# Attention state in three column strips, border factors multiplied behind their transfer, scores cut at the causal mask

## The chip, the core and the metric

The kernel runs on one core of a Trainium2 chip. The metric is the device time in microseconds of one execution. TensorE is called PE here (its weight loads PEld), VectorE DVE, ScalarE ACT, GpSimd POOL, and SyncE, which issues all transfers, SP.

## What is computed

Three layers in a row. The first is a gated attention of 4 batches with 8 heads, 768 steps and a head size of 48. The other two are dense layers on the 3072 tokens (384 to 2048 to 384 with an elu, and 384 to three times 768, maximum, to 384). The change touches the first alone:

```python
S_re, S_im = 0, 0                        # a 48x48 state per head, complex
for t in range(S):
    new_re = ar * S_re - ai * S_im       # ar, ai: a_re, a_im with their length cut to 0.999
    new_im = ar * S_im + ai * S_re
    S_re, S_im = (new_re + k[t] (x) v[t], new_im)
    y[:, :, t] = q[t] @ S_re
```

## The kernel before

The steps of a batch are cut into 6 chunks of 128; two neighbouring chunks of all 8 heads are one group n (12 groups), its chunks c = 0 and 1, the second with its steps in reverse order. In a chunk the recurrence becomes matrix products. Phases and log lengths are summed over the steps, and from them come `ep` and `em` (exponentials of the summed log length and of its negative). `hat` (L444) turns q and k into `qh` and `kh` with 96 rows per head (cosine and sine parts).

- `score` (L499) multiplies kt and qt of each head: 128 x 128 values in a PSUM bank, four heads to a bank, so two halves `hf` per chunk. For n < PE_TR = 3 that is one matmul per head (L505). From n = 3 on the 128 key rows are four strips of 32 columns of the array (`tile_position`), because the transposed k lies in four blocks of 32 (L508). `mask` (L513) then multiplies the whole bank by `keep[c]`, which is 0 where the key is later than the query.
- `state` (L522) is one matmul per head, 96 columns of `kh` against 48 columns of v (L531). `state_out` (L540) adds it to the running state and multiplies by the factor `g`, which carries the decay over the border between two chunks.
- `gain` (L388) makes `g`: it takes the exponential `gt` of half a log length from `rate` (L382), multiplies it on DVE by `em` of the next chunk and `ep` of this one (L394, L395, on 32 partitions, though only one row is needed), writes the row to DRAM (`gd`, L398), and reads it back turned, one value per partition and head, twice (L401).
- `yout` (L554) adds masked scores times v and state times q, also in four column strips (L563).
- Scores, states, outputs and sums take their PSUM banks from `apsum` (L127): at the start of the kernel three banks "h" and two banks "a" in turn, later the two "a" alone.

Group n's steps are laid by a table (`STEPS`, L633) between the steps of the first dense layer: `h_pair` (L681) and `o_pair` (L724) give 18 + 18 matmuls per step, and `elu` and `elu_split` follow on ACT and DVE two steps behind. So PE alternates between long runs of L681 and L724 and short pieces of attention. A scheduler behind the program sets the final order on each engine; every engine works its own row strictly in that order, and SP issues all transfers in one row. The second dense layer (L928, L952) comes at the end and holds no attention.

Of the kernel before, what the change touches and what calls it, by code (L numbers as in the profile page):

```python
# [9 lines left out]
F32 = mybir.dt.float32  # L10
F32R = mybir.dt.float32r
# [3 lines left out]
AF = mybir.ActivationFunctionType  # L15
ALU = mybir.AluOpType
# [3 lines left out]
B, H, S, D = 4, 8, 768, 48  # L20
P = 128
W = H * D
NCH = S // P
NG = B * NCH // 2
# [9 lines left out]
NWA, NWB = 2 * DM, 3 * NK * P + DM  # L34
LAG = 2
PE_TR = 3
NCONST = 8 * P + 2
PRIO_X = 400
DEC0 = 2
RAW0 = 2  # L40
# [52 lines left out]
def tile_kernel(  # L93
# [14 lines left out]
    nc = tc.nc  # L108
    act = ActQueue(tc)
    cp = ctx.enter_context(tc.tile_pool(name="cp", bufs=1))  # L110
# [4 lines left out]
    ps = pm.enter_context(tc.tile_pool(name="ps", bufs=1, space=PSUM))  # L115
# [9 lines left out]
    early = [0, True]  # L125

    def apsum():  # L127
        if early[1]:
            early[0] += 1
            if early[0] % 5 not in (1, 3):  # L130
                return ps.tile([P, 512], F32, tag="h", name="a", bufs=3)
        return ps.tile([P, 512], F32, tag="a", name="a", bufs=2)

    def load_re(n):
        T["re", n] = at([P, 2, W], "re")
# [19 lines left out]
    sums_raw = at([P, 4 * P], "p", bufs=2)  # L155
    nc.sync.dma_start(sums_raw, consts[:, 3 * P + 2:7 * P + 2])
    sums_r = cp.tile([P, 4 * P], F32R, name="sums_r")
    nc.gpsimd.tensor_copy(sums_r, sums_raw)
    tri_l = [sums_r[:, i * P:(i + 1) * P] for i in (0, 1)]
    keep_r = [sums_r[:, i * P:(i + 1) * P] for i in (2, 3)]  # L160
    keep = [x.bitcast(F32) for x in keep_r]

    def const_col(x, name):
        t = cp.tile([P, 1], F32, name=name)
# [12 lines left out]
    gd = dp.tile([2 * NG, 1, W], F32, name="gd")  # L177

    def load_w(pool, src, f, n, tag):
        raw = pool.tile([P, n, 2], U32, tag=tag, name="raw")  # L180
# [50 lines left out]
        )  # L231
        return split_w(wpool, t, n, tag)

    s_tiles = [at([96, 4, P], f"s{i}") for i in (0, 1)]
    for s in s_tiles:
        nc.vector.memset(s, 0.0)

# [13 lines left out]
        nc.sync.dma_start(T["k", n], k[n])  # L251

    def load_v(n, c):
        T["v", n, c] = at([P, 512], "v", bufs=2)
        nc.sync.dma_start(T["v", n, c], v[n, :, c, :])

    def new(nm, n):
# [53 lines left out]
    def bslice(c):  # L311
        return slice(96, 128) if c == 0 else slice(0, 32)
# [67 lines left out]
        act.activation(em, bank[:, :W], AF.Exp, scale=-1.0)  # L380

    def rate(n):  # L382
        T["gt", n] = t = at([P, W], "gt")
        for c in (0, 1):
            sl = bslice(1 - c)
            act.activation(t[sl], T["lnr", n][sl, c, :], AF.Exp, scale=0.5)

    def gain(n, c):  # L388
        if ends(n, c):
            return  # L390
        n2, c2 = after(n, c)
        sl = bslice(c)
        t = T["gt", n2]
        nc.vector.tensor_tensor(out=t[sl], in0=t[sl], in1=T["em", n2, c2][sl], op=ALU.mult)  # L394
        nc.vector.tensor_tensor(out=t[sl], in0=t[sl], in1=T["ep", n, c][sl], op=ALU.mult)  # L395
        row = P - 1 if c == 0 else 0
        ci = 2 * n + c
        nc.sync.dma_start(gd[ci], t[row:row + 1, :])  # L398
        g = at([96, H], "g", bufs=2)
        for j in (0, 1):  # L400
            T["dma"] = nc.sync.dma_start(  # L401
                g[j * D:(j + 1) * D, :], gd[ci].rearrange("o (h d) -> d (o h)", h=H)
            )
        T["g", ci] = g

    def heads(t):
# [46 lines left out]
    def tr_pe(n, c, x, hf):  # L453

        if n >= PE_TR:
            return
        if ("qkt", n, c) not in T:
            if early[1] and c == 1:
                d = [mp.tile([96, H, P], F32, tag="g", name="qkt", bufs=LAG + 1) for _ in "qk"]
            else:  # L460
                d = at([96, 2, H, P], "qkt")
                d = [d[:, 0], d[:, 1]]
            T["qt", n, c], T["kt", n, c] = ([y[:, i, :] for i in range(H)] for y in d)
# [48 lines left out]

    def mask(n, c, hf):  # L513
        bank = T.pop(("sc", n, c, hf))
        t = at([P, 4, P], "p", bufs=2)
        T["p", n, c, hf] = t
        nc.vector.tensor_tensor(  # L517
            out=t, in0=bank.rearrange("p (i t) -> p i t", i=4),
            in1=keep[c].unsqueeze(1).to_broadcast([P, 4, P]), op=ALU.mult,
        )  # L520

    def state(n, c):  # L522
        ci = 2 * n + c
        if ends(n, c):
            return
        bank = apsum()
        kh = T["kh", n, c].rearrange("p h j d -> p h (j d)")
        vt = T["v", n, c]
        for h in range(H):
            o = (h // 2) * P + (h % 2) * 80  # L530
            nc.tensor.matmul(  # L531
                bank[:96, h * D:(h + 1) * D], lhsT=kh[:, h, :], rhs=vt[:, o:o + D],
                start=True, stop=True,
            )
        T["sps", ci] = bank

    def split_heads(t):
# [677 lines left out]
def _consts():  # L1215
    import numpy as np

    t = [np.arange(P), P - 1 - np.arange(P)]
    c = np.zeros((P, NCONST), np.float32)
    for i in (0, 1):  # L1220
        a, b = t[i][:, None], t[i][None, :]
        c[:, i * P:(i + 1) * P] = np.where(a <= b, -1 / (2 * np.pi), 0)
        m = np.zeros((P, P), np.float32)
        m[(b >= 64) & (a >= 64) & (a <= b)] = 0.5
        m[(b < 63) & (a > b) & (a <= 63)] = -0.5
        s = (3 + i) * P + 2
        c[:, s:s + P] = m
        c[:, s + 2 * P:s + 3 * P] = a <= b
    c[:, 2 * P:3 * P] = np.eye(P)
# [5 lines left out]
    return c  # L1235


def _row_perm():
# [11 lines left out]
def _layout(inputs):  # L1250
# [14 lines left out]
    vp[..., 80:96] = v[..., 1, 32:]  # L1265
    vp[..., 96:128] = v[..., 1, :32]
    a["v"] = vp.reshape(NG, P, 2, 4 * P)
# [50 lines left out]
```

## Time and profile before

| | |
|---|---|
| median of 3 runs (lowest to highest) | 940.64 us (939.47 to 941.17) |
| profiled execution, its own time | 941.66 us |
| its span | 939.7 us |
| mean granted clock of PE | 0.987 |
| PE, DVE, ACT, POOL busy | 899.0, 604.2, 536.8, 0.8 us |

Busy shares are averages over stages with different limits, so they are read by stretch. In the rows below a float32 matmul is two rows (two passes), and a matmul's length in the trace is longer than the distance to the next, since matmuls are pipelined; the distance between starts is what a matmul costs.

### The profile page before, as it was taken

The numbers are of one execution on the slowest core, as the hardware profiler recorded it, in microseconds if no ns is written. First come the engines' busy times: TensorE is split into PE (matmuls) and PEld (weight loads), VectorE is DVE, ScalarE is ACT, GpSimd is POOL, SyncE is SP. The second block draws the span as 40 slices with busy tenths as digits, with TensorE's granted clock in tenths as the row PEclk, the third lists the DMA queues.
The fourth block names the chain that finished last, engine by engine and source line by source line (L and its number), as shares of the span: only waits on it lengthen the run. The fifth ranks groups of instructions, "written<-read, shape, count | busy, mean of one in ns | idle before, by whom it ended". The sixth has DMA issues, their size and how long they took to land.

```text
span 939.7 us, 19152 instructions
## 1 busy us (share of the span) xinstructions
PE 899.0 (96%) x8036; PEld 820.3 (87%) x8036; DVE 604.2 (64%) x952; ACT 536.8 (57%) x869; POOL 0.8 (0%) x5
## 2 busy tenths in 40 slices
PE   4579999999999999999999999999999999999997
PEld 1568889999999999999999999998888889898886
DVE  6889899788777797877786743778843141322220
ACT  8868777776767675757564533655858521211111
POOL 0000000000000000000000000000000000000000
PEclk9987999999999999999999999999999999999999
DMA  8662012343333333333323221619687401000001
GB/s 312 230 244 63 1 47 80 79 114 96 81 81 96 80 97 100 78 91 86 83 62 92 51 57 42 252 39 367 220 308 277 151 2 67 1 26 9 18 17 38
DMA packets 69703, 99.41 MB, mean 106 GB/s; under 512 B 22740, under 2 KB 52584, under 8 KB 68840
## 3 DMA queue, kind: packets, MB, share of 16 engines
q1 hardware_dynamic: 69608, 98.10, 33.1%
q8 instruction: 65, 1.06, 0.5%
q14 instruction: 30, 0.25, 0.1%
HBM read 74.45 MB, written 9.47 MB: 89 GB/s over the span
## 4 chain that ended last, share of the span: by engine, by line
PE 85%; DVE 6%; ACT 4%; DMA 3%; issue 1%; SPq 0%; DVEq 0%; ACTq 0%
PE mb L928 21%; PE x L724 21%; PE h L681 20%; PE ob L952 7%; PE a L563 5%; PE a L508 4%; PE a L531 3%; DMA rng<-in_a_im_dram 2%; PE a L330 1%; PE a L505 1%; ACT rng L78 1%; PE a L468 1%; ACT L78 1%; ACT aux L78 1%; DMA g<-gd 1%
## 5 line engine op out<-in xcount | busy, mean ns | idle before, releaser
L681 PE MATMUL h<-x,w 128*128 128x256 f32 x1728 | 232.9, 286 | 4.9 <-ACT w L83 2.5
L724 PE MATMUL x<-g,w 128*128 128x256 f32 x1728 | 230.3, 286 | 1.8 <-ACT x L83 1.4
L681 PEld LDWEIGHTS h<-x,w 128*128 128x128 f32 x1728 | 217.9, 192 | 11.4 <-ACT w L83 3.4
L928 PE MATMUL mb<-xx,w 128*128 128x512 f32 x972 | 224.8, 392 | 0.0
L724 PEld LDWEIGHTS x<-g,w 128*128 128x128 f32 x1728 | 215.3, 191 | 9.8 <-issue 6.9
L928 PEld LDWEIGHTS mb<-xx,w 128*128 128x128 f32 x972 | 182.4, 188 | 40.8
L78 ACT ACTIVATE e<-h 128x512 f32<-128x512 f32 x96 | 57.1, 595 | 104.8 <-PE h L681 104.8
L692 DVE SCALAR_TENSOR_TENSOR e<-e,h 128x512 f32<-128x512 f32 x96 | 65.1, 678 | 42.5 <-ACT e L78 42.0
L83 ACT CAST g<-e 128x512 fp32r<-128x512 f32 x96 | 59.4, 618 | 52.1 <-DVE e L692 51.7
L936 DVE TENSOR_TENSOR t<-mb,t 128x512 f32<-128x512 f32 x36 | 24.8, 689 | 96.1 <-PE mb L928 96.1
L701 DVE TENSOR_TENSOR g<-e,g 128x512 fp32r<-128x512 f32 x96 | 65.7, 685 | 18.8 <-ACT g L83 18.4
L952 PE MATMUL ob<-w,m 128*128 128x384 f32 x432 | 76.7, 337 | 0.1
L952 PEld LDWEIGHTS ob<-w,m 128*128 128x128 f32 x432 | 75.5, 188 | 0.9 <-ACT o L83 0.4
L83 ACT CAST m<-t 128x512 fp32r<-128x512 f32 x36 | 22.3, 620 | 92.1 <-DVE t L937 92.0
L78 ACT ACT_TABLE_LOAD x54 | 69.3, 1283 | 1.7 <-PEq L1302 0.8
L78 ACT ACTIVATE e<-e 128x512 f32<-128x512 f32 x96 | 60.6, 633 | 2.2
L937 DVE TENSOR_TENSOR t<-mb,t 128x512 f32<-128x512 f32 x36 | 24.9, 690 | 34.6 <-PE mb L928 34.5
L517 DVE TENSOR_TENSOR p<-a,sums_r 128x512 f32<-128x512 f32 x48 | 32.6, 683 | 10.7 <-PE a L508 8.1
L940 DVE TENSOR_TENSOR m<-t,m 128x512 fp32r<-128x512 f32 x36 | 24.8, 690 | 22.7 <-ACT m L83 22.7
L508 PE MATMUL a<-qkt 96*32 96x128 f32 x1152 | 38.9, 276 | 0.0
L83 ACT COPY o<-ob 128x384 f32<-128x384 f32 x24 | 11.4, 476 | 45.4 <-PE ob L952 45.3
L563 PE MATMUL a<-p,v 128*32 128x128 f32 x768 | 35.1, 283 | 0.3 <-DVE p L517 0.2
(106 smaller groups left out, 986.8 us busy)
## 6 DMA issues: line engine op xcount, KB each, us to landing
qkt<-tb SPq DMA_DIRECT2D x216, 64.0 KB
raw<-in_wa_dram SPq DMA_DIRECT2D x16, 768.0 KB
again<-in_wa_dram SPq DMA_DIRECT2D x16, 768.0 KB
raw<-in_wb_dram SPq DMA_DIRECT2D x6, 1536.0 KB
v<-in_v_dram SPq DMA_DIRECT2D x24, 256.0 KB
q<-in_q_dram SPq DMA_DIRECT2D x12, 384.0 KB
k<-in_k_dram SPq DMA_DIRECT2D x12, 384.0 KB
x2d<-x SPq DMA_DIRECT2D x36, 128.0 KB
```

What stands on the lines that cost most here:

```text
L78: ins = self.nc.scalar.activation(out, in_, func, **k)
L83: self.nc.scalar.copy(out, in_)
L508: nc.tensor.matmul(o[32 * s:32 * s + 32], lhsT=k1[:, s], rhs=q1, start=True, stop=True, tile_position=(0, 32 * s),)
L517: nc.vector.tensor_tensor(out=t, in0=bank.rearrange("p (i t) -> p i t", i=4), in1=keep[c].unsqueeze(1).to_broadcast([P, 4, P]), op=ALU.mult,)
L531: nc.tensor.matmul(bank[:96, h * D:(h + 1) * D], lhsT=kh[:, h, :], rhs=vt[:, o:o + D], start=True, stop=True,)
L563: nc.tensor.matmul(bank[32 * quad:32 * quad + 32, o * P:(o + 1) * P], lhsT=lhs, rhs=rhs, start=start, stop=stop, tile_position=(0, 32 * quad),
L681: nc.tensor.matmul(bank[:, i * BT:(i + 1) * BT], lhsT=w[:, wi, wsl], rhs=xb[b][:, xi, kk, :], start=m == 0, stop=m == 8,)
L692: nc.vector.scalar_tensor_tensor(out=e, in0=e, scalar=-1.0, in1=bank, op0=ALU.add, op1=ALU.max)
L701: nc.vector.tensor_tensor(out=g[:, 1], in0=e, in1=g[:, 0].bitcast(F32), op=ALU.subtract)
L724: nc.tensor.matmul(x2[m], lhsT=w[:, wi, wsl], rhs=g[:, gi, i * BT:(i + 1) * BT], start=j + i + s == 0 and b > 1, stop=j == NP - 1 and i == ...
L928: nc.tensor.matmul(bank, lhsT=wbt[f][:, wt, o:o + P], rhs=x[:, xi, kk].rearrange("p c t -> p (c t)"), start=m == 0, stop=m == 8,)
L952: nc.tensor.matmul(bank[:, :DM], lhsT=mt[:, mi, ts], rhs=wbt[f][:, wt, NWB - DM:], start=f == 0 and s == 0, stop=f == NF2 - 1 and s == 2,)
```

## The change

1. **State.** Each head's 96 columns of `kh` become three column strips of 32, with their own `tile_position`. The values v of odd heads, which `state` reads, lie in a place of their own behind the 512 columns of a v tile (704 columns).
2. **Border factors.** The rows of `em`, `ep` and the rate are written to `gd` one by one, read back turned in one transfer per half (3 x 8 values per partition), and multiplied there, on 96 x 8 values. The rate lies in 32 unused partitions of the state tiles.
3. **Scores.** All groups use strips. From n = 1 on a strip is as wide as the mask keeps it: for c = 0 strip f has queries f to 3, for c = 1 queries 0 to f (in blocks of 32). In odd heads the key blocks stand in reverse order in the columns, with the mask and v's rows reversed to match, and the strips are issued in the order 0, 3, 1, 2 or 3, 0, 2, 1.
4. **Banks.** What a strip does not write stays as it was in the bank and is multiplied by 0 in `mask`. So the two banks "a" are kept for good (`apsum_a`), and two matmuls set them to zero at the start.

```diff
     def apsum():
...
-        return ps.tile([P, 512], F32, tag="a", name="a", bufs=2)
+        return apsum_a()
+
+    def apsum_a():
+
+        if not banks_a:
+            banks_a.extend(ps.tile([P, 512], F32, tag="a", name="a", bufs=2) for _ in (0, 1))
+        banks_a.reverse()
+        return banks_a[0]
...
-    s_tiles = [at([96, 4, P], f"s{i}") for i in (0, 1)]
+    s_full = [at([P, 4, P], f"s{i}") for i in (0, 1)]
+    s_tiles = [s[:96] for s in s_full]
+    rates = [s.rearrange("p a t -> p (a t)")[96:128, :W] for s in s_full]
...
     def load_v(n, c):
-        T["v", n, c] = at([P, 512], "v", bufs=2)
+        T["v", n, c] = at([P, NV], "v", bufs=2)
...
     def rate(n):
-        T["gt", n] = t = at([P, W], "gt")
         for c in (0, 1):
-            sl = bslice(1 - c)
-            act.activation(t[sl], T["lnr", n][sl, c, :], AF.Exp, scale=0.5)
+            act.activation(rates[c], T["lnr", n][bslice(1 - c), c, :], AF.Exp, scale=0.5)

     def gain(n, c):
...
-        nc.vector.tensor_tensor(out=t[sl], in0=t[sl], in1=T["em", n2, c2][sl], op=ALU.mult)
-        nc.vector.tensor_tensor(out=t[sl], in0=t[sl], in1=T["ep", n, c][sl], op=ALU.mult)
-        row = P - 1 if c == 0 else 0
+        row, off = (P - 1, 31) if c == 0 else (0, 0)
         ci = 2 * n + c
-        nc.sync.dma_start(gd[ci], t[row:row + 1, :])
-        g = at([96, H], "g", bufs=2)
+        for i, x in enumerate((T["em", n2, c2], T["ep", n, c])):
+            nc.sync.dma_start(gd[ci, i:i + 1], x[row:row + 1, :])
+        nc.sync.dma_start(gd[ci, 2:3], rates[c2][off:off + 1, :])
+        f = at([96, 3, H], "f", bufs=2)
         for j in (0, 1):
             T["dma"] = nc.sync.dma_start(
-                g[j * D:(j + 1) * D, :], gd[ci].rearrange("o (h d) -> d (o h)", h=H)
+                f[j * D:(j + 1) * D], gd[ci].rearrange("o (h d) -> d o h", h=H)
             )
+        g = at([96, H], "g", bufs=2)
+        nc.vector.tensor_tensor(out=g, in0=f[:, 0], in1=f[:, 1], op=ALU.mult)
+        nc.vector.tensor_tensor(out=g, in0=g, in1=f[:, 2], op=ALU.mult)
...
     def score(n, c, hf):
...
-            o, k1, q1 = bank[:, i * P:(i + 1) * P], kt[4 * hf + i], qt[4 * hf + i]
-            if n < PE_TR:
-                nc.tensor.matmul(o, lhsT=k1, rhs=q1, start=True, stop=True)
-                continue
-            for s in range(4):
+            k1, q1 = kt[4 * hf + i], qt[4 * hf + i]
+            for s in (0, 3, 1, 2) if (i + c) % 2 == 0 else (3, 0, 2, 1):
+                f = s if i % 2 == 0 else 3 - s
+                a, b = (0, 4) if n == 0 else (f, 4) if c == 0 else (0, f + 1)
                 nc.tensor.matmul(
-                    o[32 * s:32 * s + 32], lhsT=k1[:, s], rhs=q1, start=True, stop=True,
+                    bank[32 * s:32 * s + 32, i * P + 32 * a:i * P + 32 * b],
+                    lhsT=k1[:, f], rhs=q1[:, a:b], start=True, stop=True,
                     tile_position=(0, 32 * s),
                 )
...
     def state(n, c):
...
-            o = (h // 2) * P + (h % 2) * 80
-            nc.tensor.matmul(
-                bank[:96, h * D:(h + 1) * D], lhsT=kh[:, h, :], rhs=vt[:, o:o + D],
-                start=True, stop=True,
-            )
+            o = (h // 2) * P if h % 2 == 0 else 4 * P + (h // 2) * D
+            for j in range(3):
+                sl = slice(32 * j, 32 * j + 32)
+                nc.tensor.matmul(
+                    bank[sl, h * D:(h + 1) * D], lhsT=kh[:, h, sl], rhs=vt[:, o:o + D],
+                    start=True, stop=True, tile_position=(0, 32 * j),
+                )
...
         nc.tensor.matmul(t, lhsT=zero[:, :P], rhs=zero, start=True, stop=False)
+    for t in (apsum_a(), apsum_a()):
+        nc.tensor.matmul(t, lhsT=zero[:, :P], rhs=zero, start=True, stop=True)
```

Three places show how the instructions stand before and after. On PE, a half of the scores of n = 3 between two runs of the dense layer, before:

```order
L724 MATMUL x_1966<-g,w 128x256 x3
L724 MATMUL x_1967<-g,w 128x256 x3
L508 MATMUL a<-qkt 32x128 x16
L330 MATMUL a<-gs,sums_r 128x384 x2
L724 MATMUL x_1968<-g,w 128x256 x3
```

and after, the first of its four heads (the other three repeat the four widths):

```order
L742 MATMUL x_119<-g,w 128x256 x3
L742 MATMUL x_120<-g,w 128x256 x3
L742 MATMUL x_121<-g,w 128x256 x3
L522 MATMUL a<-qkt 32x128
L522 MATMUL a<-qkt 32x32
L522 MATMUL a<-qkt 32x96
L522 MATMUL a<-qkt 32x64
```

The same 16 matmuls stand at the same place, with 128, 32, 96 and 64 columns in place of 128 each.

On PE, a state of a later group, before:

```order
L508 MATMUL a<-qkt 32x128 x16
L681 MATMUL h<-x,w 128x256 x18
L531 MATMUL a<-v,kh 96x48 x8
L563 MATMUL a<-p,v 32x128 x4
L563 MATMUL a<-qkt,s_101 32x128 x4
```

and after:

```order
L742 MATMUL x_121<-g,w 128x256 x3
L549 MATMUL a<-v,kh 32x48 x24
L699 MATMUL h<-x,w 128x256 x18
L742 MATMUL x_119<-g,w 128x256 x3
L742 MATMUL x_120<-g,w 128x256 x3
```

Eight matmuls of 96 weight columns became 24 of 32, and here they stand alone between runs of the dense layer.

On DVE, around the border factor of a later group (`s` is the running state, L551/L569 adds to it and L552/L570 multiplies by g), before:

```order
L517 TENSOR_TENSOR p<-a,sums_r 128x512
L692 SCALAR_TENSOR_TENSOR e<-e,h 128x512
L394 TENSOR_TENSOR gt<-gt,em_4163 32x384
L551 TENSOR_TENSOR s_100<-a,s_101 96x4x2x48
L395 TENSOR_TENSOR gt<-gt,ep_4079 32x384
L701 TENSOR_TENSOR g<-e,g 128x512
L552 TENSOR_TENSOR s_100<-s_100,g 96x4x2x48
```

and after:

```order
L532 TENSOR_TENSOR p<-a,sums_r 128x512
L415 TENSOR_TENSOR g<-f 96x8
L710 SCALAR_TENSOR_TENSOR e<-e,h 128x512
L416 TENSOR_TENSOR g<-g,f 96x8
L453 TENSOR_TENSOR q<-q,ep_4421 128x384
L453 TENSOR_TENSOR k<-k,em_4422 128x384
L569 TENSOR_TENSOR s_103<-a,s_104 96x4x2x48
L719 TENSOR_TENSOR g<-e,g 128x512
L570 TENSOR_TENSOR s_103<-s_103,g 96x4x2x48
```

L394 and L395 stood ahead of a transfer whose result a later L552 used. L415 and L416 stand behind the transfer whose result L570 uses here, and L415, the first to wait for it, is five operations ahead of L569.

## Rows read from the trace of the kernel before

**Rows 1.** The page, part 1: busy us, share of the span, instructions.

```profile
PE 899.0 (96%) x8036; PEld 820.3 (87%) x8036; DVE 604.2 (64%) x952; ACT 536.8 (57%) x869; POOL 0.8 (0%) x5
```

**Rows 2.** Stretches: length; PE, PEld, DVE, ACT, POOL busy (count); granted clock; DMA share; GB/s.

```profile
0.00:200.00 200.00, 166.03 (x1491) 146.23 (x1492) 170.55 (x271) 152.83 (x231) 0.81 (x5) 0.95 0.39 131
200.00:633.40 433.40, 433.40 (x5142) 416.37 (x5142) 321.72 (x519) 267.58 (x427) 0.00 (x0) 1.00 0.32 87
633.40:939.70 306.30, 299.62 (x1406) 257.66 (x1404) 111.90 (x162) 116.34 (x214) 0.00 (x0) 0.99 0.32 115
```

**Rows 3.** The chain that ended last, its share by engine.

```profile
PE 85%; DVE 6%; ACT 4%; DMA 3%; issue 1%; SPq 0%; DVEq 0%; ACTq 0%
```

**Rows 4.** PE in order of time, one score half: start us, length us, line, shapes, count.

```profile
191.66 1.08 PE L508 MATMUL a<-qkt 96*32 96x128 f32 x32
192.68 0.39 PE L724 MATMUL x<-g,w 128*128 128x256 f32 x1
```

**Rows 5.** The same from 191.66, windows ending at 191.70, 191.82, 191.93; PEld at 191.80.

```profile
191.46 0.28 PE L724 MATMUL x<-g,w 128*128 128x256 f32 x1
191.66 0.32 PE L508 MATMUL a<-qkt 96*32 96x128 f32 x4
191.66 0.43 PE L508 MATMUL a<-qkt 96*32 96x128 f32 x8
191.66 0.54 PE L508 MATMUL a<-qkt 96*32 96x128 f32 x12
191.66 0.16 PEld L508 LDWEIGHTS a<-qkt 96*32 96x32 f32 x8
```

**Rows 6.** L508's group (busy us, mean ns); stretches with L508 alone, then L531 alone.

```profile
L508 PE MATMUL a<-qkt 96*32 96x128 f32 x1152 | 38.9, 276 | 0.0
0.00:200.00 200.00, 2.16 (x64) 1.62 (x64) 0.95 0.39 131
200.00:633.40 433.40, 36.75 (x1088) 27.62 (x1088) 1.00 0.32 87
...
0.00:200.00 200.00, 10.92 (x96) 10.91 (x96) 0.95 0.39 131
200.00:633.40 433.40, 20.86 (x224) 20.53 (x224) 1.00 0.32 87
```

**Rows 7.** Chain in order of time, one run of the dense layer: start us, us, what.

```profile
163.26 2.15 PE x L724 x18
```

**Rows 8.** PE in order of time, one state; between, the window ending at 222.53.

```profile
222.48 1.48 PE L531 MATMUL a<-v,kh 128*96 128x48 f32 x16
223.78 0.61 PE L724 MATMUL x<-g,w 128*128 128x256 f32 x3
...
222.48 0.29 PE L531 MATMUL a<-v,kh 128*96 128x48 f32 x2
```

**Rows 9.** PE in order of time, a score half of n = 2.

```profile
138.16 1.06 PE L505 MATMUL a<-qkt 96*128 96x128 f32 x8
138.97 0.60 PE L681 MATMUL h<-x,w 128*128 128x256 f32 x3
```

**Rows 10.** DVE groups: shapes, count, busy us, mean ns, idle before.

```profile
L394 DVE TENSOR_TENSOR gt<-gt,em 32x384 f32<-32x384 f32 x20 | 11.0, 549 | 0.4
L395 DVE TENSOR_TENSOR gt<-gt,ep 32x384 f32<-32x384 f32 x20 | 11.0, 549 | 0.4
...
L1016 DVE SCALAR_TENSOR_TENSOR flags<-flags,sums 128x24 f32<-128x24 f32 x1 | 0.2, 184 | 4.1 <-ACT rng L78 4.1
```

**Rows 11.** Reads of g: chain at the start; PE's wait; SP and DVE around 175 us.

```profile
37.63 6.16 DMA g<-gd
...
44.52 3.75 PE L505 MATMUL a<-qkt 96*128 96x128 f32 x16 [4.31 <-DVE s L548]
...
174.15 2.08 SPq L401 DMA_DIRECT2D g<-gd  x2
...
178.08 0.55 DVE L548 TENSOR_TENSOR s<-a,g 96x384 f32<-96x384 f32 x1 [0.71 <-DMA g<-gd]
```

More of the change, by code (lines that the diff above doesn't have):

```diff
@@ L36 @@
 PE_TR = 3
-NCONST = 8 * P + 2
+NCONST = 10 * P + 2
+NV = 4 * P + 4 * D
 PRIO_X = 400
@@ L123, in at @@
         return ap.tile(shape, dt, tag=tag, name=name or tag, bufs=bufs)
-    early = [0, True]
+    early, banks_a = [0, True], []
     def apsum():
@@ L154, in tile_kernel @@
     wrap_at = cst[:, 3 * P:3 * P + 2]
[L155 to L161, printed above, removed]
+    sums_r = cp.tile([P, 6, P], F32R, name="sums_r")
+    for i in (0, 2):
+        raw = at([P, 4 * P], "p", bufs=2)[:, :(4 - i) * P]
+        a, b = (3 * P + 2, 7 * P + 2) if i == 0 else (8 * P + 2, 10 * P + 2)
+        nc.sync.dma_start(raw, consts[:, a:b])
+        nc.gpsimd.tensor_copy(sums_r[:, i + i:4 + i].rearrange("p a t -> p (a t)"), raw)
+    tri_l = [sums_r[:, i] for i in (0, 1)]
+    keep_r = [sums_r[:, i] for i in (2, 3)]
+    keep = [
+        sums_r[:, 2 + c::2].bitcast(F32).unsqueeze(1).to_broadcast([P, 2, 2, P]) for c in (0, 1)
+    ]
     def const_col(x, name):
@@ L176, in tile_kernel @@
     x2d = dp.tile([NT // P, P, NK * P], F32, name="x2d")
-    gd = dp.tile([2 * NG, 1, W], F32, name="gd")
+    gd = dp.tile([2 * NG, 3, W], F32, name="gd")
     def load_w(pool, src, f, n, tag):
@@ L391, in gain @@
         n2, c2 = after(n, c)
-        sl = bslice(c)
-        t = T["gt", n2]
-        nc.vector.tensor_tensor(out=t[sl], in0=t[sl], in1=T["em", n2, c2][sl], op=ALU.mult)
-        nc.vector.tensor_tensor(out=t[sl], in0=t[sl], in1=T["ep", n, c][sl], op=ALU.mult)
-        row = P - 1 if c == 0 else 0
+        row, off = (P - 1, 31) if c == 0 else (0, 0)
         ci = 2 * n + c
-        nc.sync.dma_start(gd[ci], t[row:row + 1, :])
-        g = at([96, H], "g", bufs=2)
+        for i, x in enumerate((T["em", n2, c2], T["ep", n, c])):
+            nc.sync.dma_start(gd[ci, i:i + 1], x[row:row + 1, :])
+        nc.sync.dma_start(gd[ci, 2:3], rates[c2][off:off + 1, :])
+        f = at([96, 3, H], "f", bufs=2)
         for j in (0, 1):
             T["dma"] = nc.sync.dma_start(
-                g[j * D:(j + 1) * D, :], gd[ci].rearrange("o (h d) -> d (o h)", h=H)
+                f[j * D:(j + 1) * D], gd[ci].rearrange("o (h d) -> d o h", h=H)
             )
+        g = at([96, H], "g", bufs=2)
+        nc.vector.tensor_tensor(out=g, in0=f[:, 0], in1=f[:, 1], op=ALU.mult)
+        nc.vector.tensor_tensor(out=g, in0=g, in1=f[:, 2], op=ALU.mult)
         T["g", ci] = g
@@ L462, in tr_pe @@
                 d = [d[:, 0], d[:, 1]]
-            T["qt", n, c], T["kt", n, c] = ([y[:, i, :] for i in range(H)] for y in d)
+            T["qt", n, c], T["kt", n, c] = (
+                [y[:, i, :].rearrange("p (s t) -> p s t", s=4) for i in range(H)] for y in d
+            )
             T["qkt", n, c] = d
@@ L517, in mask @@
         nc.vector.tensor_tensor(
-            out=t, in0=bank.rearrange("p (i t) -> p i t", i=4),
-            in1=keep[c].unsqueeze(1).to_broadcast([P, 4, P]), op=ALU.mult,
+            out=t.rearrange("p (i e) t -> p i e t", e=2),
+            in0=bank.rearrange("p (i e t) -> p i e t", i=2, e=2),
+            in1=keep[c], op=ALU.mult,
         )
@@ L529, in state @@
         for h in range(H):
-            o = (h // 2) * P + (h % 2) * 80
-            nc.tensor.matmul(
-                bank[:96, h * D:(h + 1) * D], lhsT=kh[:, h, :], rhs=vt[:, o:o + D],
-                start=True, stop=True,
-            )
+            o = (h // 2) * P if h % 2 == 0 else 4 * P + (h // 2) * D
[4 more added lines that the diff above has]
+                    start=True, stop=True, tile_position=(0, 32 * j),
+                )
         T["sps", ci] = bank
@@ L1228, in _consts @@
         c[:, s + 2 * P:s + 3 * P] = a <= b
+        c[:, (8 + i) * P + 2:(9 + i) * P + 2] = (a <= b)[_blocks()]
     c[:, 2 * P:3 * P] = np.eye(P)
@@ L1235, in _consts, with _blocks @@
     return c
+def _blocks():
+    import numpy as np
+    return np.arange(P).reshape(4, 32)[::-1].reshape(P)
 def _row_perm():
@@ L1264, in _layout @@
     vp[..., 0:48] = v[..., 0, :]
-    vp[..., 80:96] = v[..., 1, 32:]
-    vp[..., 96:128] = v[..., 1, :32]
-    a["v"] = vp.reshape(NG, P, 2, 4 * P)
+    odd = np.concatenate([v[..., 1, 32:], v[..., 1, :32]], axis=-1)
+    vp[..., 80:128] = odd[:, _blocks()]
+    a["v"] = np.concatenate(
+        [vp.reshape(NG, P, 2, 4 * P), odd.reshape(NG, P, 2, 4 * D)], axis=-1
+    )
     w_in = inputs["moe_w_in"][_row_perm()].reshape(NK, P, NF1, P).transpose(1, 2, 0, 3)
```

## The prediction

> **What bounds the kernel now.** I read the busy shares first: PE is busy for 899.0 of 939.7 us [rows 1]. An average over stages can hide a different limit in one of them, so the second view cuts the span in three. From 200 to 633.4 us PE is busy 433.40 of 433.40 us with a granted clock of 1.00 (the 2.4 GHz level), while DVE is busy 321.7 and ACT 267.6. Before 200 us PE has 166.0 of 200 and DVE 170.6. After 633.4 us nothing that the change touches is left [rows 2]. The chain that ended last is 85% PE and 6% DVE [rows 3]. So from 200 us on, a microsecond of PE work removed is a microsecond of the time, as long as PE stays the latest. Before 200 us DVE and transfers count as much as PE.
>
> The sums are made against the profiled execution, 941.66 us for a span of 939.7; that is 1.0 us above the median of the three runs, 940.64, so the result has 1.0 us taken off.
>
> **The score strips (L508).** A half of a chunk's scores is 4 heads x 4 strips x 2 rows, since each float32 matmul appears as two rows of the trace. One half: the last ordinary matmul starts at 191.46, L508 at 191.66, the next line at 192.68 [rows 4, 5]. Inside, four matmuls have started by 191.70, eight by 191.82, twelve by 191.93 [rows 5]: the four strips, which lie in four column groups, run side by side, in rounds. The last start is at 191.66 + 1.08 - 0.28 = 192.46 [rows 4, 6], so the 8 rounds are 0.81/7, about 0.11 us apart, 0.88 in all; the other 0.14 of the 1.02 us is the fill at the start and the way out. Ordinary rows follow each other every 2.15/18 = 0.12 us [rows 7]. L508 starts 0.08 later than that after its predecessor, and the way out after the last round costs 0.10: some 0.19 us for going into the strips and back.
>
> After the change a strip has 128, 96, 64 or 32 columns, and the next head gives the long strip to the column group that had the short one. Over two heads each group gets 4 + 1 or 3 + 2 blocks of 32 columns, twice: 10 blocks where it had 16. If each group works at its own pace and its time goes by columns, 0.88 becomes 0.55; I take 0.57, because short strips leave some weight loads uncovered. Saved per half: 0.31 us. No row shows a four-group burst with fewer than 128 columns, so this is bounded: from 0.33 saved to nothing saved (the feed, first rival). I take the upper part because a group's second matmul does not hold up its neighbours: the first round's four starts and all 8 weight loads of two rounds lie within 0.16 us [rows 5], and a 48-column row of L531 is followed by the next start within 0.05 us where the weights are there already [rows 8]. There are 1088 rows from 200 us on [rows 6], 34 halves of 32: 34 x 0.31 = 10.5 us, and 2 halves before that, 0.6.
>
> The groups n < 3 had whole 128x128 scores: 8 rows, 0.81 us to the next line [rows 9], 0.93 with the 0.12 before. As strips for n = 1 and 2 they cost 0.20 to enter + 0.57 + 0.14 = 0.91: nothing. For n = 0 the strips are full: 0.20 + 1.02, which is 0.29 more for each of 4 halves, at a place where PE waits anyway. I count zero; with no cover it is +1.2.
>
> **The state (L531).** Before: 16 rows of 96 weight columns, 1.30 us from first start to the next line [rows 8]; the starts are 1.30/16, about 0.08, apart although a 48-column row needs 0.05 or less: the weights set the pace. After: 48 rows in three column groups, 16 one after the other in each, at 48/128 x 0.11 = 0.042 us: 0.67, plus fill and way out 0.14, plus 0.09 for going in: 0.90. Saved: 0.40 each. Before, this matmul needed no change into column groups, so here the change adds 20 such returns at 0.19. The Trainium skill, page "TensorEngine Tiling (Array Packing)", section "Key Properties", speaks against this edit too: changing the tiling mode drains the engine. It gives no price; rows 4 and 5 do, and the 0.40 is what is left after paying it. The 224 rows after 200 us [rows 6] are 14 calls: 5.6 us. Of the 6 before, three lie where PE is nearly full (after 100 us): 1.2. Per call the bounds are 0.49 saved (no way in to pay, where it stands next to other strips) and 0.17 lost (first rival).
>
> **The border factors (L394, L395).** Two DVE operations of 550 ns go, 20 times each: 22 us. Two on 96x8 come; the nearest row is 184 ns for 128x24 [rows 10], so 7.4 us. From 200 us on DVE has over 100 us free, so 0. Before that 6 of the 20 are affected: 6 x 0.73 = 4.4 us of DVE work, of which I count 2.5, since PE or transfers are the later ones in part of it.
>
> Each factor now makes three small writes instead of one, and each of the two reads has 24 elements per partition instead of 8. They leave on SP's queue, in front of the loads of q, k, v and, at the start, of eight weight tiles. The new DVE operations wait for this read, and everything behind them on DVE waits too: the carry into th, the weight decode, e and g of the elu. Bounds: a read landed 6.16 us after its issue when the weight tiles followed it, and within 1.9 us (issued until 176.23, used at 178.08) elsewhere [rows 11]. Three times the elements takes between the same and three times as long: +0 to +12.3 at the start, +0 to +3.8 elsewhere. Against this, the writes no longer wait for two DVE operations (1.1 us), and the order puts the multiplications three or more DVE operations before the first use. At the start PE waited 4.31 us for L548 [rows 11]; in the new order the scores of the second chunk stand ahead of that wait. I take +1.5 at the start and 0 elsewhere. The wider v loads (704 columns for 512) and the two zeroing matmuls lie beside idle queues and an idle PE in the first 15 us: 0; uncovered they would be under 2 us each.
>
> **Sum.** -10.5 - 0.6 - 5.6 - 1.2 - 2.5 + 1.5 = -18.9 on 941.66, or 922.8; less 1.0 is 921.8, which I give as **922 us**.
>
> **Rivals.**
> *The feed.* In rows 4 the 32 matmuls start over 0.81 us, 0.026 each. The same number would come out if PE could not feed a weight load and a matmul faster than one pair in 0.026 us, whatever the columns. Then a score half saves nothing, a state is 48 x 0.026 + 0.23 = 1.47 for 1.30, and the halves of n = 1, 2 cost 0.29 more each: +0.17 x 17 + 0.29 x 12 - 2.5 + 1.5 = +5.4 at the most, about +2 with what PE idle covers before 200 us: 943. The edits together break even at some 0.025 us a pair. For it: the coincidence of the numbers. Against it: the first starts in rows 5, far closer together. A page has the same rule: the Trainium skill, "TensorE: Matmul & The Clock Gate", section "Wait — 56ns, not 53.3ns?", says that start to start never drops below about 25 ns however small the matmul. By that rule the result is about 941; the four starts within 0.04 us [rows 5] disagree for different column groups, and no run here shows it for a long burst. Chance 17%.
> *The read stalls DVE (slower).* If the read's time triples, the first one lands 12.3 us later and the other five before 200 us some 2.9 us later (3.8 less part of the 1.1), where DVE has little room: +27 against -17.9: about 950. It turns the sign once the six waits come to 18 us, 3 us each. For it: the only long wait for g in the trace is there. Against it: the reads go out before the weight loads and SP finds the rows ready earlier. Chance 12%.
> *PE is no longer last.* With 16 us less PE work from 200 us on, DVE is at 322 - 10 of 417 us, 75%, but in order, and e and g wait for ACT. If half of the gain is taken by such waits: 930. Chance 13%.
> The forecast has the other 58%.
>
> **How the numbers follow.** The forecast's own spread, from the bounds of the two PE terms and of the start, is 913 to 929. The range reaches up over the partial case and the feed to 943 and leaves out the stalled read and a little below: **913 to 943**. About 0.2%, 1.9 us, is what a measurement can tell from no change. Faster by more: forecast 58 + partial 13 + 4 of the feed's 17 = 75%. Within: 10% of the feed's. Slower: 12 + 3 = 15%.
>
> **What would show it.** Right: a score half (L522) goes from 1.02 us to about 0.70 from its first start to the next line, a state (L549) from 1.30 to about 0.81 with 0.20 before it, and the stretch from the first full PE window to the end of the h and x stage is 16 us shorter with PE still full. Feed: starts in L522 keep a mean of 0.026 us and L549 takes about 1.4 us. Stalled read: DVE rows of L415 with waits of several us for f. Wrong altogether: PE idle time in the stage that is full now, or a granted clock below 1.00 there.

## The result

The changed kernel takes 925.04 us (median of 4 runs, 923.73 to 925.48); the kernel before, on the same chip, 940.9. The ratio is 0.9838, with a 95% interval of 0.982 to 0.9855. The profiled execution took 924.66 us for a span of 922.9, so 17.0 us less than the one before, where the forecast was 18.9 less.

These lines of the profile after answer to [rows 1 to 3]: busy shares, the three stretches (the second ends where the dense stage ends now), and the chain that ended last.

```profile
PE 879.2 (95%) x8968; PEld 797.4 (86%) x8968; DVE 584.8 (63%) x952; ACT 535.8 (58%) x869; POOL 1.2 (0%) x6
...
0.00:200.00 200.00, 165.92 (x2001) 141.10 (x2002) 166.68 (x276) 153.45 (x233) 1.15 (x6) 0.94 0.46 143
200.00:616.50 416.50, 413.95 (x5565) 398.56 (x5564) 306.23 (x515) 266.47 (x424) 0.00 (x0) 1.00 0.37 92
616.50:922.90 306.40, 299.34 (x1406) 257.71 (x1404) 111.88 (x162) 115.90 (x214) 0.00 (x0) 0.99 0.32 115
...
PE 81%; ACT 9%; DVE 6%; issue 1%; SPq 1%; DMA 1%; DVEq 0%; ACTq 0%
```

PE is busy 19.8 us less, and the third stretch is as long as it was: all of the gain lies ahead of it. But PE is no longer busy for the whole of the second stretch: 2.55 us of it are idle, where there were none.

A score half and a state after 200 us, PE in order of time (start us, length us), answer to [rows 4] and [rows 8]:

```profile
226.62 0.76 PE L522 MATMUL a<-qkt 96*32 96x128 f32 x32
227.31 0.39 PE L742 MATMUL x<-g,w 128*128 128x256 f32 x1
...
219.52 0.88 PE L549 MATMUL a<-v,kh 128*32 128x48 f32 x48
220.34 0.51 PE L742 MATMUL x<-g,w 128*128 128x256 f32 x2
```

From the first start to the next line a half takes 0.69 us (1.02 before), a state 0.82 (1.30). Counted from the start of the ordinary matmul ahead to the start of the one behind, a half is 0.900 where it was 1.220, and a state 1.02 where it was 1.42; 28 of the stage's 34 halves and 12 of its 14 states show these figures to 0.01 us (33 and 11 in the trace of before).

The multiplications of the border factors, by group (count, busy us, mean ns, idle before them), answer to [rows 10] and [rows 11]:

```profile
L415 DVE TENSOR_TENSOR g<-f 96x8 f32<-96x8 f32 x20 | 3.1, 157 | 3.6 <-DMA f<-gd 3.5 <-issue 0.2
L416 DVE TENSOR_TENSOR g<-g,f 96x8 f32<-96x8 f32 x20 | 3.0, 148 | 0.0
```

In all 20 uses together DVE waited 3.5 us for the wider read.

Where PE is idle between 200 and 300 us (the bracket gives the idle time and what ended it):

```profile
209.68 0.84 PE L549 MATMUL a<-v,kh 128*32 128x48 f32 x45 [1.21 <-ACT em L79]
...
274.20 0.76 PE L522 MATMUL a<-qkt 96*32 96x128 f32 x32 [0.67 <-DVE nr L364]
...
278.38 0.45 PE L344 MATMUL a<-gs,sums_r 128*128 128x384 f32 x1 [0.62 <-DVE gs L334]
```

Each is a wait for the gate chain of a later group (angles, cumulative sums, their exponentials) on ACT and DVE.

### The profile page after: what moved, and what is told of

It is laid out like the page before. It is cut to its first block, busy times and chain, and to the rows that moved or that the text cites. A ratio compares the mean times of both kernels' runs of the same rounds, so it can differ in the third digit from the quotient of the medians.

```text
span 922.9 us, 21089 instructions
## 1 busy us (share of the span) xinstructions
PE 879.2 (95%) x8968; PEld 797.4 (86%) x8968; DVE 584.8 (63%) x952; ACT 535.8 (58%) x869; POOL 1.2 (0%) x6
## 4 chain that ended last, share of the span: by engine, by line
PE 81%; ACT 9%; DVE 6%; issue 1%; SPq 1%; DMA 1%; DVEq 0%; ACTq 0%
PE mb L948 24%; PE x L742 19%; PE h L699 18%; PE ob L972 8%; PE a L581 4%; PE a L522 3%; ACT L79 3%; ACT aux L79 1%; PE a L549 1%; PE a L344 1%; ACT e L79 1%; SPq L508 1%; ACT m L79 1%; PE a L483 1%; ACT g L84 1%
## 5 line engine op out<-in xcount | busy, mean ns | idle before, releaser
L742 PE MATMUL x<-g,w 128*128 128x256 f32 x1728 | 230.4, 286 | 0.5 <-DVE g L719 0.5
L948 PE MATMUL mb<-xx,w 128*128 128x512 f32 x972 | 224.8, 392 | 0.0
L742 PEld LDWEIGHTS x<-g,w 128*128 128x128 f32 x1728 | 215.1, 191 | 6.6 <-issue 3.8
L948 PEld LDWEIGHTS mb<-xx,w 128*128 128x128 f32 x972 | 182.4, 188 | 40.8
L522 PE MATMUL a<-qkt 96*32 96x128 f32 (+3 forms) x1536 | 38.0, 244 | 3.0 <-ACT qkt L84 2.3
L522 PEld LDWEIGHTS a<-qkt 96*32 96x32 f32 x1536 | 32.3, 112 | 9.5 <-ACT qkt L84 2.6
```

The lines of the kernel that those rows point to most:

```text
L522: nc.tensor.matmul(bank[32 * s:32 * s + 32, i * P + 32 * a:i * P + 32 * b], lhsT=k1[:, f], rhs=q1[:, a:b], start=True, stop=True, tile_pos ...
L742: nc.tensor.matmul(x2[m], lhsT=w[:, wi, wsl], rhs=g[:, gi, i * BT:(i + 1) * BT], start=j + i + s == 0 and b > 1, stop=j == NP - 1 and i == ...
L948: nc.tensor.matmul(bank, lhsT=wbt[f][:, wt, o:o + P], rhs=x[:, xi, kk].rearrange("p c t -> p (c t)"), start=m == 0, stop=m == 8,)
```

## Experiments

Four kernels ran beside each other in each of three groups, each group on one chip beside the kernel before. I compare by the ratio to the kernel before; 0.001 is 0.94 us. The kernel after, run again, gives the ratio to compare with: 0.9842 (0.9824 to 0.9859). The intervals reach 1.1 to 1.9 us either way, so differences of 1 or 2 us between two kernels are not clear of them.

### What sets the time of a score half

*Full strips* (kernel after, nothing skipped):

```diff
-                a, b = (0, 4) if n == 0 else (f, 4) if c == 0 else (0, f + 1)
+                a, b = 0, 4
```

> The kernel after, but every score strip is 128 columns wide again (nothing is skipped; the reversed blocks, the state in three strips and the new factors stay). Own pace: each column group runs through its own queue and its time goes by its columns, so a half (L522) goes from 0.69 us back to about 1.01 from its first start to the next line; 34 halves from 200 us on give +10.9 us, less up to 2.5 us of PE idle time between 200 and 300 us that slower scores would cover, and 8 halves of n = 1, 2 add 0 to 2.5: 933.5 to 938 us. Feed (the number of weight loads sets the time and the columns do not): halves stay near 0.69, 925 us.

Measured: 938.43 us, ratio 0.9989 (0.9975 to 1.0003). *No reversal* (skipping kept, but one column group has all the long strips; the layout of v and the mask follow):

```diff
-                f = s if i % 2 == 0 else 3 - s
+                f = s
...
-    vp[..., 80:128] = odd[:, _blocks()]
+    vp[..., 80:128] = odd
```

> The kernel after with the skipped columns, but odd heads are not reversed, so that one column group has the long strip (128 columns) of all four heads of a half and another the short one (32). The number of columns is that of the kernel after. Own pace: the slowest group has 16 blocks of 32 columns where it had 10, a half takes about 1.0 us again and the whole gain of the scores goes: 933.5 to 938 us, as in the run with full strips. Shared stream (the sum of the columns over all groups sets the time): a half stays at 0.69 us, 925 us.

Measured: 935.92 us, ratio 0.9973 (0.9961 to 0.9985). One half of each, PE in order of time, full strips first:

```profile
341.87 1.08 PE L522 MATMUL a<-qkt 96*32 96x128 f32 x32
342.88 1.34 PE L699 MATMUL h<-x,w 128*128 128x256 f32 x9
```

```profile
340.27 1.06 PE L522 MATMUL a<-qkt 96*32 96x128 f32 x32
341.26 1.94 PE L699 MATMUL h<-x,w 128*128 128x256 f32 x14
```

1.01 us with full strips, 0.99 with as many columns as in the kernel after but unevenly spread, 0.69 in the kernel after. With the sum of columns setting the time, the second would have been 0.69. So the busiest column group decides: 16 blocks of 32 columns in either slow case, 10 in the kernel after. The feed falls with the same rows, since the number of strips is the same in all three. By the ratios the first run is 0.0147, or 13.8 us, above the kernel after. 44 halves are affected (34 after 200 us, 10 before): 44 x 0.32 = 14.1, less 1.0 us that PE is idle less between 200 and 300 us, is 13.1. The second is 12.3 above: 44 x 0.30 = 13.2, less 1.5, is 11.7. The first is a little above what was expected, the second in its upper part; the sums fit if the halves before 200 us count in full.

*Order of issue* (kernel after, strips of each head issued as 0, 1, 2, 3):

```diff
-            for s in (0, 3, 1, 2) if (i + c) % 2 == 0 else (3, 0, 2, 1):
+            for s in range(4):
```

> The kernel after, but the four strips of every head are issued in the order 0, 1, 2, 3 where the kernel after changes the order from head to head; which group has which width is the same. If a group takes its next strip as soon as it is free, wherever that stands in the program: a half stays at 0.69 us, and the time at 0.984 of before. If strips have to start in the order of the program, a short strip waits behind the long one of the next head in another group: a half takes 0.75 to 1.0 us, 3 to 12 us more.

Measured: 929.59 us, ratio 0.989 (0.9877 to 0.9904), 4.5 us above the kernel after. The first theory is right about the half and wrong about the time. A half that stands in one piece takes 0.91 us from start to start instead of 0.90, so strips do not wait in the order of the program. But the scheduler, which here orders PE's rows anew, cut four of the 48 halves into 12 pieces with dense work between. One of them, in order of time:

```profile
294.81 0.25 PE L522 MATMUL a<-qkt 96*32 96x32 f32 x2
294.99 0.98 PE L699 MATMUL h<-x,w 128*128 128x256 f32 x6
295.90 0.30 PE L522 MATMUL a<-qkt 96*32 96x64 f32 x2
296.13 1.09 PE L699 MATMUL h<-x,w 128*128 128x256 f32 x7
297.15 0.35 PE L522 MATMUL a<-qkt 96*32 96x96 f32 x2
297.43 0.38 PE L699 MATMUL h<-x,w 128*128 128x256 f32 x1
...
298.34 0.75 PE L522 MATMUL a<-qkt 96*32 96x128 f32 x26
299.02 0.38 PE L742 MATMUL x<-g,w 128*128 128x256 f32 x1
```

The four pieces cost 0.39 + 0.44 + 0.49 + 0.89 = 2.21 us from start to start; less 0.90 for a whole half and three ordinary spacings of 0.12, each cut costs 0.32. Eight cuts are 2.5 us and 34 x 0.01 another 0.3; the other 1.7 I did not trace.

### The state

*Whole state* (kernel after, 96 weight columns at a time):

```diff
-            for j in range(3):
-                sl = slice(32 * j, 32 * j + 32)
...
-                    bank[sl, h * D:(h + 1) * D], lhsT=kh[:, h, sl], rhs=vt[:, o:o + D],
-                    start=True, stop=True, tile_position=(0, 32 * j),
+            nc.tensor.matmul(
+                bank[:96, h * D:(h + 1) * D], lhsT=kh[:, h, :], rhs=vt[:, o:o + D],
```

> The kernel after, but the state is one matmul with 96 weight columns per head again, as before. If the three strips give 0.40 us per call (0.81 + 0.21 us against 1.30 + 0.12): +5.6 us for the 14 calls from 200 us on, 0 to +2 for those earlier, less what PE idle time between 200 and 300 us swallows: 928 to 932.5 us. If the return into column groups eats it, or if PE waits elsewhere for as long: 924 to 926.

Measured: 928.07 us, ratio 0.9892 (0.9875 to 0.991), 4.7 us above the kernel after; a state is as before, and PE's idle time between 200 and 300 us is 1.36 us:

```profile
217.48 1.48 PE L547 MATMUL a<-v,kh 128*96 128x48 f32 x16
218.78 2.40 PE L740 MATMUL x<-g,w 128*128 128x256 f32 x18
...
200.00:300.00 100.00, 98.64 (x1246) 94.53 (x1248) 77.77 (x137) 70.72 (x109) 0.00 (x0) 1.00 0.39 91
```

14 x 0.40 = 5.6, less the 1.2 us that PE is idle less, is 4.4 for the 4.7 measured: the strips' gain is real, and part of it had turned into waits.

### The border factors

*Old factors* (kernel after, multiplied before the transfer, in the tile that holds the rates now):

```diff
-        for i, x in enumerate((T["em", n2, c2], T["ep", n, c])):
-            nc.sync.dma_start(gd[ci, i:i + 1], x[row:row + 1, :])
+        nc.vector.tensor_tensor(out=t, in0=t, in1=T["em", n2, c2][sl], op=ALU.mult)
+        nc.vector.tensor_tensor(out=t, in0=t, in1=T["ep", n, c][sl], op=ALU.mult)
+        nc.sync.dma_start(gd[ci], t[off:off + 1, :])
...
-        nc.vector.tensor_tensor(out=g, in0=f[:, 0], in1=f[:, 1], op=ALU.mult)
-        nc.vector.tensor_tensor(out=g, in0=g, in1=f[:, 2], op=ALU.mult)
```

> The kernel after, but the border factors are multiplied before the transfer again (two DVE operations on 32 x 384, one row written, 8 elements per partition read). By the forecast's steps (-2.5 us of DVE work before 200 us, +1.5 for the read at the start) this is +1.0: 924.5 to 927.5 us. If the 3 us that are missing to the forecast were lost to the larger transfers or to the waits of DVE for them: 922 to 923.5 us.

Measured: 924.26 us, ratio 0.9851 (0.9833 to 0.9869): 0.8 us above the kernel after, inside the intervals. That fits the forecast's +1.0, but it would fit no difference as well; the places do not agree. PE busy in three stretches, old factors first, then the kernel after:

```profile
0.00:100.00 100.00, 75.10 (x895) 55.77 (x896) 84.95 (x136) 81.14 (x118) 1.21 (x6) 0.91 0.57 206
100.00:200.00 100.00, 92.94 (x1102) 86.69 (x1101) 87.86 (x141) 74.97 (x118) 0.00 (x0) 0.97 0.29 79
200.00:300.00 100.00, 99.80 (x1444) 95.22 (x1447) 83.80 (x140) 72.91 (x114) 0.00 (x0) 1.00 0.34 88
```

```profile
0.00:100.00 100.00, 69.17 (x844) 50.08 (x845) 81.83 (x135) 75.52 (x113) 1.15 (x6) 0.88 0.60 207
100.00:200.00 100.00, 96.75 (x1160) 91.02 (x1159) 84.85 (x142) 77.94 (x122) 0.00 (x0) 1.00 0.32 79
200.00:300.00 100.00, 97.49 (x1399) 92.96 (x1398) 78.64 (x138) 71.87 (x112) 0.00 (x0) 1.00 0.37 88
```

With the new factors PE is busy 5.9 us less in the first 100 us, 3.8 more in the second, and 2.3 less in the third. Busy time is not progress where the clock differs (0.91 and 0.88, 0.97 and 1.00 here), so I also compare the starts of one row: the first x matmul starts at 75.21 us with old factors and at 82.38 in the kernel after, the 289th at 182.44 and 185.09, the first of the last stage at 615.17 and 616.30. The old factors start earlier and lose most of the lead again by 200 us. The idle time between 200 and 300 us goes with the new factors: with the same fast strips and old factors it is 0.20 us.

*New factors alone* (kernel before, only the factors changed):

```diff
-        nc.vector.tensor_tensor(out=t[sl], in0=t[sl], in1=T["em", n2, c2][sl], op=ALU.mult)
-        nc.vector.tensor_tensor(out=t[sl], in0=t[sl], in1=T["ep", n, c][sl], op=ALU.mult)
+        for i, x in enumerate((T["em", n2, c2], T["ep", n, c])):
+            nc.sync.dma_start(gd[ci, i:i + 1], x[row:row + 1, :])
```

> The kernel before with the new border factors alone (three rows written as they come, 24 elements per partition read, the two multiplications on 96 x 8 behind). By the forecast's steps -1.0 us against before (-2.5 of DVE work, +1.5 at the start): -3 to +0.5. If the factors cost at the start what they give between 100 and 200 us: within 1 us of before, with the marks at 100 us later than before and the difference gone by 200 us. If the larger reads hold DVE up: +3 us or more, and waits of several us for f.

Measured: 943.27 us (940.54 to 947.43 in 8 runs), ratio 1.0039 (1.002 to 1.0059): 3.4 us slower than before, outside the forecast's range. That is the size of the third case but not its cause: the waits for f are 6.1 us in 6 places, the longest 1.7. The profiled execution was the fastest of the eight, 1.1 us under the profile of before, so it does not show where the others lose. One number exists for all: the granted clock, averaged over the span, was 0.982 in the mean of the eight, against 0.989 in the mean of the 13 of the kernel before beside them. What part of the 3.4 us that is stays open; the mean clock does not order the kernels, for it was 0.981 in the next one, the fastest of its group.

*Two early old factors* (kernel after; n = 0 as in the run with old factors):

```diff
+    def gain_0(n, c):
...
+        if 2 * n + c < 2:
+            gain_0(n, c)
+        else:
+            gain_1(n, c)
```

> The kernel after, but the first two border factors (n = 0) are multiplied before the transfer, as before, and all later ones behind it. In the run with old factors throughout, the first elu work began 4 to 5 us earlier than in the kernel after and the lead was gone by 200 us, which I put down to the 549 ns multiplications that stand in DVE's way there. If so, this keeps the early start without the later loss: 2 to 5 us faster than the kernel after. If the early start came from the order of the whole program, or if DVE takes it back whatever the factors: within 1 us.

Measured: 922.22 us (920.95 to 923.82), ratio 0.9809 (0.9791 to 0.9826). The kernel after beside it: 925.02 (923.87 to 927.02), 0.9842 (0.9824 to 0.9859). That is 2.8 us faster, at the low end of what was expected, and the intervals only just touch. *The wide read alone* (that kernel, its two early factors still multiplied first, but written three times and read with 24 elements):

```diff
-        nc.sync.dma_start(gd[ci, 0:1], t[off:off + 1, :])
-        g = at([96, H], "g", bufs=2)
+        for i in range(3):
+            nc.sync.dma_start(gd[ci, i:i + 1], t[off:off + 1, :])
+        f = at([96, 3, H], "f", bufs=2)
...
```

> The kernel with the early old factors (0.981 of before), whose two early border factors are still multiplied before the transfer, but three rows are written and 24 elements per partition read for them, as in the kernel after; the program reads the first 8. This is the price of the wider transfers at the start by itself, apart from when the multiplications stand. By the forecast's +1.5 us: 0.9825 of before. If the read is what costs the kernel after its start: 0.984, with a wait of several us for f in the first use. If the width costs nothing: 0.981, and the first use waits no longer than with 8 elements.

Measured: 921.46 us (920.08 to 922.99), ratio 0.9809 (0.9795 to 0.9822): the width costs nothing that can be measured. With intervals of 1.3 and 1.7 us either way the times alone do not exclude the forecast's +1.5; the trace has to say whether anything waited. The first read and its first use on DVE, with no wait ahead of it:

```profile
34.73 1.04 SPq L411 DMA_DIRECT2D f<-gd  x2
...
43.06 0.55 DVE L588 TENSOR_TENSOR s<-a,f 96x384 f32<-96x384 f32 x1
43.52 0.94 DVE L216 TENSOR_TENSOR w<-dt,w 128x768 fp32r<-128x768 f32 x1
```

In the kernel after, the same place on DVE:

```profile
44.26 0.15 DVE L415 TENSOR_TENSOR g<-f 96x8 f32<-96x8 f32 x1
...
44.86 0.15 DVE L416 TENSOR_TENSOR g<-g,f 96x8 f32<-96x8 f32 x1
...
45.81 0.54 DVE L566 TENSOR_TENSOR s<-a,g 96x384 f32<-96x384 f32 x1
...
47.15 0.95 DVE L216 TENSOR_TENSOR w<-dt,w 128x768 fp32r<-128x768 f32 x1
```

Nothing waits for the transfer here either. But the state update and the first weight tile stand 2.8 and 3.6 us later, behind weight decoding that came after them in the other order, and the first h starts at 50.58 us where it starts at 46.35 in the run with the wide read. So at the start it is the order on DVE that costs, and the transfer makes nothing wait.

*The kernel after again*, unchanged:

> The kernel after, unchanged, beside the other three on one chip, so that differences of 1 to 3 us can be read. Every theory: 0.9838 of the kernel before (0.982 to 0.9855). If the PE idle time between 200 and 300 us and the gap of 5.7 us at 66 us are set by the order of the program, they stand at the same places again.

Measured: 925.02 us, ratio 0.9842. The gap before L549 stands in its trace again, 1.21 us for em, and PE has 97.33 of 100 us between 200 and 300. The gap at 66 us is there too, 6.96 us long where it was 5.70. These waits belong to the order.

### Whole scores at the start

*Early whole* (kernel after; scores and states of n < 3 as before, v and mask of these groups unreversed):

```diff
+            if n < PE_TR:
+                nc.tensor.matmul(
+                    bank[:, i * P:(i + 1) * P], lhsT=k1.rearrange("p s t -> p (s t)"),
+                    rhs=q1, start=True, stop=True,
+                )
+                continue
...
```

> The kernel after, but the first three groups (n < 3, up to about 200 us) have whole 128 x 128 scores and whole 96-column states, as before; odd heads are reversed from n = 3 on only. If the strips at the start are among what is missing to the forecast (the full strips of n = 0 cost 0.29 us a half, four halves): 1 to 2.5 us faster than the kernel after. If other work covers them there, as the forecast had it, and the states of n = 1, 2 give 0.40 us each: within 1 us, or up to 1.5 us slower.

Measured: 923.53 us, ratio 0.9825 (0.9805 to 0.9845): 1.5 us faster, but the intervals overlap; inconclusive. *Both*, this and the two early old factors:

```diff
+        if 2 * n + c < 2:
+            gain_0(n, c)
...
+            if n < PE_TR:
+                nc.tensor.matmul(
...
```

> The kernel after with both changes that were measured apart: the border factors of n = 0 multiplied before the transfer (2.8 us faster than the kernel after), and whole scores and whole states for n < 3 (1.5 us faster). If the two gains lie in different gaps of PE at the start they add: 0.9795 of the kernel before, about 921 us. If both only shorten the same gap: 0.981, as with the factors alone. If the order of the program decides the start and each edit shuffles it anew: anything from 0.978 to 0.985.

Measured: 926.42 us, ratio 0.9855 (0.9838 to 0.9873). *Scores only*, as both, with the state in strips throughout:

```diff
-            if n < PE_TR:
-                nc.tensor.matmul(
-                    bank[:96, h * D:(h + 1) * D], lhsT=kh[:, h, :], rhs=vt[:, o:o + D],
...
```

> As the run with both, but the state of n < 3 stays in three strips, so only the scores of n < 3 are whole. If the state strips are worth 0.40 us a call in n = 1, 2 too (four calls): 1.0 to 1.6 us faster than the run with both. If PE has idle time there that takes it up: the same within 0.8 us.

Measured: 925.45 us, ratio 0.9844 (0.983 to 0.9858), 1 us faster than both, as the first theory has it, but inside the intervals. The gains do not add: two edits that were 2.8 and 1.5 us faster alone give nothing together (1.2 us slower than the kernel after, inside the intervals). Of the three expectations of the run with both only the last is left, the order shuffled anew, and 0.9855 lies just beyond its edge.

The kernel with two early old factors beats both the kernel before and the kernel after: 922.22 us beside 939.87 and 925.02. The twin with the wide read has the same ratio on another chip.

## Why the prediction was right, and where it was off

The forecast was 922 us, the likeliest case; measured were 925.04, within 913 to 943. That range reaches up to no change at all, so lying in it says little; the rows say more.

**Bound.** Right: the third stretch is untouched, and what PE lost in work is nearly what the time lost.

**Scores.** Right. It is 0.32 us a half where 0.31 was worked out; 34 x 0.32 = 10.9 us for 10.5. Own pace is shown by the unreversed run, not only argued. The feed fell: 32 matmuls in strips start within 0.55 us, 0.018 apart, and the 48 of a state within less than 0.82, 0.017 apart at the most, both under the 0.026 of [rows 4]. The Trainium skill's rule of about 25 ns from start to start (page "TensorE: Matmul & The Clock Gate", section "Wait — 56ns, not 53.3ns?") does not hold here for matmuls that lie in different column groups.

**State.** Right: 0.40 a call. The price of going in and out of the strips, 0.19 from [rows 4], was paid as forecast: 1.02 us from start to start, of which 0.21 lie ahead of the first start. The draining that the Trainium skill names for a change of the tiling mode (page "TensorEngine Tiling (Array Packing)", section "Key Properties") fits this delay, since ordinary matmuls start 0.12 us apart; the price is smaller than the gain.

**From 200 us on.** 10.9 + 5.6 = 16.5 us less PE work, against 16.1. The step that failed is that a microsecond of PE work is a microsecond of time all along: 2.55 us of PE idle time came, nearly all between 200 and 300 us. It is the third rival, PE no longer last, at about a third of the 8 us that it had. The prediction named such idle time as the sign of being wrong altogether; it is about a sixth of the gain in this stage, and the rest came as forecast. It takes both the faster PE and the order that comes with the new factors: between 200 and 300 us PE is idle for 0 us in the trace of before, 0.79 with the new factors alone, 0.20 with the strips and the old factors, and 2.2 to 2.7 in all eight traces that have the strips of the kernel after and the new factors there. It is no wait for f. Between 190 us and the end of the first gap DVE waits for none, and in the kernel run again one wait for f, at 260 us, was 2.45 us instead of 1.35, while the two gaps behind it kept their lengths. The first gap, which ends with em, is made by the order on ACT, where m belongs to the gates of a later group. In the kernel after:

```profile
201.84 0.85 ACT L79 ACTIVATE m<-re 128x768 f32<-128x768 f32 x1 [0.46 <-DVE lnr L320]
...
209.14 0.48 ACT L79 ACTIVATE em<-a 128x384 f32<-128x384 f32 x1
```

and with old factors:

```profile
208.29 0.48 ACT L79 ACTIVATE em<-a 128x384 f32<-128x384 f32 x1
...
209.13 0.85 ACT L79 ACTIVATE m<-re 128x768 f32<-128x768 f32 x1
```

The same 0.85 us stand ahead of em in the one and behind it in the other. Net, the gain from 200 us on is 14.0 by this sum. Read from the rows themselves it is 14.2: the first row of L948 starts at 616.30 us, 16.9 us earlier than its counterpart in the trace of before (L928, 633.20), and the 289th row of L742, at 185.09 us, 2.7 earlier.

**Before 200 us.** The sum came out (-2.8 forecast; -2.7 at that row, and -1.8 to -4.2 at the rows of L742 from 180 to 200 us, since the two orders differ), but its working was wrong. The +1.5 for the read was a wait for the transfer: DVE waited 3.5 us for f in the whole run, and not at all at the first use. What came in its place is an order on DVE in which the first weight tile stands 3.6 us later than in the run with the wide read, and the first h 4.2. A long gap of PE comes with this order:

```profile
71.89 1.09 PE L483 MATMUL a<-cst,qh 128*96 128x128 f32 x4 [5.70 <-ACT em L79]
```

It waits for em. With the two early old factors it is not there, though PE then waits 4.2 us for s near the same time. And PE's idle time before 200 us is, taken together, what it was (34.1 us, 34.0 before). The -2.5 for DVE's relief was not measured by itself. The lead of the old factors, 7.2 us at the first x, is 2.7 at 185 us, so the new ones give back about 4.5 there, and this too comes with another order. That errors on both sides nearly cancel is luck; with the kernel before around them, the same factors alone were 3.4 us slower. The wider v loads and the two zeroing matmuls, which were counted as nothing, were not run apart.

**The read stalls DVE.** Did not happen: no wait for f is longer than 1.4 us (2.45 in the kernel run again).

So of the 3 us between 922 and 925.04, the two profiled executions show 1.9 (17.0 us gained for 18.9), and all of it lies after 200 us: 2.55 us of idle time, less 0.4 that the strips gave beyond the forecast. The rest is how the profiled executions stand to their medians: that of before 1.0 us above the median that the forecast used, that of the kernel after 0.4 below its own.

## What to carry to other kernels

When small matmuls lie side by side in column groups, count the columns of the busiest group: skipping work pays only if every group skips as much, and here the reversal of every other head was nearly the whole of the scores' gain (0.99 us a half without it, 0.69 with it, 1.02 before). Keep such a burst in one piece, since each cut into it cost 0.32 us. An edit that touches the order of a full program has an effect of its own, here about 3 us either way; it can't be had from durations, so give it room in the range, and try the edit's parts one by one, as one of them may be better left out at the start.

## What was not expected of the hardware

Column groups run ahead of the program's order: with strips issued in the order 0, 1, 2, 3 a half in one piece took 0.91 us from start to start, 0.01 more than with a changing order, although a long strip then stands ahead of a short one of another group. The run without reversal shows it directly. These rows, by width, have started in the first 0.13 us of its half at 340.27 us:

```profile
L522 PE MATMUL a<-qkt 96*32 96x96 f32 x2 | 0.4, 258 | 0.0
L522 PE MATMUL a<-qkt 96*32 96x32 f32 x4 | 0.3, 201 | 0.0
L522 PE MATMUL a<-qkt 96*32 96x64 f32 x2 | 0.3, 232 | 0.0
L522 PE MATMUL a<-qkt 96*32 96x128 f32 x1 | 0.3, 297 | 0.0
```

A head has two rows of each width, and the strip of 128 columns is the first head's first. Four rows of 32 columns, those of two heads, have started while the second row of that strip has not. So the strict order of an engine's row, of which the section on the kernel before speaks, does not hold on PE across column groups.

The granted clock falls to the lower level (0.50, 1.2 GHz) around 70 to 80 us in both kernels, with idle time of PE ahead of it. Columns as in [rows 2], before, then after:

```profile
60.00:70.00 10.00, 5.44 (x36) 4.35 (x36) 9.81 (x14) 8.11 (x13) 0.00 (x0) 0.92 0.26 58
70.00:80.00 10.00, 9.05 (x57) 8.30 (x56) 8.61 (x14) 8.78 (x12) 0.00 (x0) 0.50 0.17 52
...
60.00:70.00 10.00, 4.94 (x48) 4.38 (x48) 9.94 (x14) 5.16 (x9) 0.00 (x0) 0.75 0.19 36
70.00:80.00 10.00, 4.57 (x54) 3.18 (x58) 8.04 (x14) 9.93 (x15) 0.00 (x0) 0.50 0.27 42
```

Averaged over the span it was 0.983 in the mean of the five runs of the kernel after, run again, and 0.989 in that of the kernel before beside it. An edit that makes PE wait at the start may thus also make the work behind it slower; how much of the time that is, no run here shows.
